# Sliding-window attention feeding a tanh MLP: attention stages spread over half-slots, and the second batch's V loaded later

## The chip, the cores and the metric

One Trainium2 chip, one core. The metric is the device time of one execution in microseconds. A profiled execution gives a trace; its span runs from the first to the last instruction and is a little shorter than the device time.

## The reference, cut to what matters

Eight batches of eight heads, 576 tokens, head size 64. Each token attends to itself and the 63 tokens before it. The attention output, with the heads side by side, is 4608 tokens of 512 channels; it goes through `w_in` (512 x 2048), `h - tanh(h)`, and `w_out` (2048 x 512).

```
B, H, S, D = 8, 8, 576, 64
rel  = pos[:, None] - pos[None, :]
mask = (rel >= 0) & (rel < 64)
attn = softmax(where(mask, q @ k.T / sqrt(D), -1e9))
x    = (attn @ v).transpose(0, 2, 1, 3).reshape(B * S, H * D)
h    = x @ w_in
out  = (h - tanh(h)) @ w_out
```

## The kernel before

**Attention** goes by pairs of heads: `g` counts 32 pairs, four to a batch (`b, pr = divmod(g, 4)`). For one pair: `load_qk` (SP queue) fetches q and k in f32, `cast_qk` (GpSimd) makes bf16 rows, and `tr` transposes them on TensorE (8 transposes for q, 8 for k). For q, ScalarE and then VectorE copy the two halves from PSUM into `qT`; for k ScalarE copies all into `kT`. The 576 queries are nine windows of 64, in three groups of three: `scores(g, grp)` is three matmuls into a PSUM tile and one Exp on ScalarE into `PT`; `masking(g)` is one VectorE multiply over all nine; `pv(g, grp)` is three matmuls with V (whose 129th column of ones gives the row sums) into the one PSUM buffer `ov`, then on VectorE a reciprocal and two multiplies into `xs`. After every second pair `x_tr` transposes four, then five windows of `xs` on TensorE, and VectorE copies them into `xT`, the MLP's input. `kT`, `qT` and `PT` have three buffers each, the transposes' PSUM tile `tp` two.

V sits in `vw` (two buffers, for two batches): `load_v(b)` (GpSimd queue) writes the upper 64 partitions with a cast to bf16, and `shift_v(b)` (SP queue) copies them on the chip to the lower 64 partitions one window further on, so that one matmul sees 128 keys. `pv` needs both.

**The MLP** goes by chunks of 512 tokens (`c` = 0 to 8), 16 steps to a chunk; `n` counts steps over all chunks. A step has `hp_mm(c, m)`: four matmuls with `w_in` into a PSUM tile `hp` (two buffers), Tanh on ScalarE, and the subtraction into `gT` on VectorE; and `yp_mm(c - 1, m)`: four matmuls with `w_out` for the chunk before. Every four steps `y_out` copies a finished `yp` (one PSUM buffer) on ScalarE and stores it. Chunk 0 (n = 0 to 15) has no `yp`, chunk 9 (n = 144 to 159) no `hp`. A chunk is eight windows and a batch nine, so chunk `c` needs the first windows of batch `c` (for c below 8) besides those left of the batch before.

**The order** is written by hand and each engine runs its instructions in that order. At step `n`: `y_out`, `hp_mm`, what stands in the table `early` for this step, `yp_mm`, what stands in `late`. Pair `g` starts at step `a` (from batch 1 on every four steps) and takes five steps: transposes at `a`, scores at `a+1`, mask and first `pv` at `a+2`, the other `pv` at `a+3`, `x_tr` at `a+4`. Mask and first `pv` are neighbours, and so are each `pv` and the `hp` or `yp` between them. Ahead of the loop stand the loads of the first batch: SP has q and k of four pairs and two `shift_v`; GpSimd's queue has V of batch 0, casts and `w_in` in quarters. V of batch 1 comes at step -8, `w_out` in quarters at steps -3 to 0, between casts.

Of the kernel before, what the change touches and what calls it, by code (L numbers as in the profile page):

```python
# [15 lines left out]
def kernel(  # L16
# [11 lines left out]
    NP = H // 2  # L28
    NJ = S // 64
# [6 lines left out]
    NC = NT // TOK  # L36
    M = d_ff // 128
# [17 lines left out]
    mask = const.tile([128, 64], BF16, name="mask")  # L55
# [19 lines left out]
    def cast(eng, g, n):  # L75
        t = row_pool.tile([P, E, 2, D], BF16, tag=n + "b", name=n + "b")
        o = t.rearrange("p e h d -> p h e d")
        i = stage.pop((g, n)).rearrange("p h (e d) -> p h e d", d=D)
        if eng is nc.scalar:
            nc.scalar.activation(o, i, ACT.Copy)  # L80
        else:
            eng.tensor_copy(o, i)  # L82
        rows[g, n] = t

    def cast_qk(g):
        cast(nc.gpsimd, g, "q")
        cast(nc.gpsimd, g, "k")

    def load_v(b, p0=0, p1=NP):
        for i in range(2):  # L90
            nc.gpsimd.dma_start(  # L91
                out=vw[b % NV][64:128, p0:p1, :, 64 * i:64 * i + 64].rearrange("p r j d -> p (r j) d"),
                in_=v[b, NP * i + p0:NP * i + p1].rearrange("h (j p) d -> p (h j) d", p=64))

    def shift_v(b, p0=0, p1=NP):
        w = vw[b % NV].rearrange("p r j c -> p r (j c)")
        nc.sync.dma_start(out=w[0:64, p0:p1, 129:], in_=w[64:128, p0:p1, :(NJ - 1) * 129])
# [23 lines left out]
    def load_w_in(i):  # L121
        nc.gpsimd.dma_start(out=w_in_sb[:, :, 512 * i:512 * i + 512],
                            in_=w_in_r[:, :, 512 * i:512 * i + 512])

    def load_w_out(i):
        nc.gpsimd.dma_start(out=w_out_sb[:, 4 * i:4 * i + 4, :], in_=w_out_r[:, 4 * i:4 * i + 4, :])

    cast(nc.scalar, 0, "q")
    cast(nc.vector, 0, "k")
    shift_v(0, 0, 1)  # L130
    load_v(0, 1, NP)
    cast_qk(1)
    load_w_in(0)
    cast_qk(2)
    shift_v(0, 1, NP)
    load_w_in(1)
    cast_qk(3)
    load_w_in(2)
    load_w_in(3)

    xT = {}

    def chunk_tile(c):
        if c not in xT:
            xT[c] = xt_pool.tile([128, 4, TOK], BF16, tag="xT", name="xT")
        return xT[c]
# [60 lines left out]
    def hp_mm(c, m):  # L207
        hp = ps_hp.tile([128, TOK], F32, tag="hp", name="hp")
        for ki in range(4):
            nc.tensor.matmul(hp, w_in_sb[:, ki, m * 128:(m + 1) * 128], chunk_tile(c)[:, ki, :],  # L210
                             start=(ki == 0), stop=(ki == 3))
        th = sm_pool.tile([128, TOK], F32, tag="th", name="th")
        nc.scalar.activation(th, hp, ACT.Tanh)  # L213
        if m == 0:
            gT[c] = g_pool.tile([128, M, TOK], BF16, tag="gT", name="gT")
        nc.vector.tensor_tensor(gT[c][:, m, :], hp, th, ALU.subtract)  # L216

    def yp_mm(c, st):
        s, part = divmod(st, 4)
        if part == 0:  # L220
            yps[c, s] = ps_yp.tile([128, d_model], F32, tag="yp", name="yp")
        for i in range(4):
            m = 4 * part + i
            nc.tensor.matmul(yps[c, s], gT[c][:, m, s * 128:(s + 1) * 128], w_out_sb[:, m, :],  # L224
                             start=(m == 0), stop=(m == M - 1))

    def y_out(c, s):
        ysb = sm_pool.tile([128, d_model], F32, tag="ysb", name="ysb")
        nc.scalar.activation(ysb, yps[c, s], ACT.Copy)  # L229
        for u in range(2):  # L230
            r0 = c * TOK + s * 128 + 64 * u
            nc.sync.dma_start(out=out[r0:r0 + 64, :].rearrange("(a e) d -> e a d", e=E),
                              in_=ysb[64 * u:64 * u + 64, :])


    early, late = {}, {}

    def at(table, n, *fn):
        table.setdefault(n, []).append(fn)

    NG = B * NP
    LEAD = 18
    for g in range(NG):
        b, pr = divmod(g, NP)
        a = g - 10 if g < NP else 4 * g - LEAD
        if g >= NP:
            at(late, a - 10, load_qk, g)
            at(late, a - 4, cast_qk, g)
        at(early, a, tr, g, "q")
        at(late, a, tr, g, "k")  # L250
        at(early, a + 1, scores, g, 0)
        at(early, a + 1, scores, g, 1)
        at(late, a + 1, scores, g, 2)
        at(early, a + 2, masking, g)
        at(late, a + 2, pv, g, 0)
        at(early, a + 3, pv, g, 1)
        at(late, a + 3, pv, g, 2)
        if pr % 2 == 1:
            at(early, a + 4, x_tr, b, pr // 2, 0, 4)
            at(late, a + 4, x_tr, b, pr // 2, 4, NJ)  # L260
    at(late, -8, load_v, 1)
    at(late, -4, shift_v, 1)
    for i in range(4):
        at(late, -3 + i, load_w_out, i)
    for b in range(2, B):
        a = 4 * (NP * (b - 1) - 1) - LEAD + 4
        at(late, a, load_v, b)
        at(late, a + 9, shift_v, b)

    first = min(min(early), min(late))  # L270
    for n in range(first, 16 * (NC + 1) + 1):
        c, m = divmod(n, M)
        cy, sy = divmod(n - 17, M)
        if n >= 17 and sy % 4 == 3 and cy < NC:
            y_out(cy, sy // 4)
        if 0 <= c < NC:
            hp_mm(c, m)
        for fn in early.get(n, []):
            fn[0](*fn[1:])
        if 1 <= c <= NC:  # L280
            yp_mm(c - 1, m)
        for fn in late.get(n, []):
            fn[0](*fn[1:])

# [1 line left out]
_INS = ['q', 'k', 'v', 'moe_w_in', 'moe_w_out']  # L286
# [26 lines left out]
```

## Time and profile before

| | |
|---|---|
| median of three runs | 490.1 us (489.14 to 490.3) |
| profiled execution, device time | 490.18 us |
| its span | 488.4 us |
| busy: TensorE, VectorE, ScalarE, GpSimd | 356.4, 237.4, 183.5, 91.2 us |
| mean granted TensorE clock | 0.967 |

Busy times are shares of the whole span; the kernel has four parts that differ: a start, in which loads and the first batch's attention run, chunk 0, the middle (n = 16 to 111), in which the MLP and the attention share the engines, and the end, which is MLP alone.

### The profile page before, as it was taken

The page shows a single profiled execution, that of the slowest core. Times are in us where ns is not written, and L with a number is a line of the kernel's source. Part 1 is how long each engine was busy: PE and PEld are TensorE (multiplying, and loading weights), DVE is VectorE, ACT ScalarE, POOL GpSimd, SP SyncE. Part 2 cuts the span into 40 slices and gives each one's busy share as a digit, 9 for nine tenths or more (in the row PEclk, how much of TensorE's full clock was granted, in tenths as well). Part 3 has the DMA queues.
Part 4 walks back from the last instruction along what each step waited for, and adds up shares of the span by engine and source line. Part 5 has one row for each costly group of instructions (what it writes and reads, how often), then busy time and mean ns, then how long its engine had stood idle before and what let it go on. Part 6 is the DMA issues. An engine that isn't in the chain of part 4 may idle for free.

```text
span 488.4 us, 6341 instructions
## 1 busy us (share of the span) xinstructions
PE 356.4 (73%) x2384; PEld 175.4 (36%) x2384; DVE 237.4 (49%) x553; ACT 183.5 (38%) x342; POOL 91.2 (19%) x97
## 2 busy tenths in 40 slices
PE   3024516765778787878787878887877879999985
PEld 2023303433333333333333333333333334444432
DVE  5036414445465656565555565655556555333410
ACT  5122203333344444435344434344444443443410
POOL 7604402103102211231123111311111000000000
PEclk9999999577899999999999999999999999999999
DMA  9999999505954495369629962996222011101112
GB/s 171 113 181 185 108 158 157 130 0 21 29 93 92 81 110 99 86 90 99 110 75 96 93 114 70 101 89 114 70 71 74 19 31 35 36 30 44 43 43 64
DMA packets 58765, 41.84 MB, mean 86 GB/s; under 512 B 38768, under 2 KB 42864, under 8 KB 58736
## 3 DMA queue, kind: packets, MB, share of 16 engines
q0 software_dynamic: 41376, 8.91, 62.7%
q1 hardware_dynamic: 17360, 32.54, 29.0%
q8 instruction: 18, 0.29, 0.3%
q14 instruction: 11, 0.09, 0.1%
HBM read 36.70 MB, written 9.44 MB: 94 GB/s over the span
## 4 chain that ended last, share of the span: by engine, by line
PE 49%; DVE 20%; DMA 13%; ACT 12%; issue 4%; POOL 1%; SPq 1%; ACTq 0%; POOLq 0%
PE hp L210 23%; PE yp L224 15%; DVE gT L216 10%; ACT th L213 8%; DMA vw<-in_v_dram 7%; PE ov L180 4%; DVE xs L186 4%; DVE pt L173 4%; ACT ysb L229 3%; DMA vw<-vw 3%; PE sp L167 3%; PE tp L153 3%; DMA kf<-in_k_dram 3%; DVE xT L200 1%; PE tpx L192 1%
## 5 line engine op out<-in xcount | busy, mean ns | idle before, releaser
L216 DVE TENSOR_TENSOR gT<-hp,th 128x512 bf16<-128x512 f32 x144 | 99.6, 692 | 153.7 <-ACT th L213 153.7
L213 ACT ACTIVATE th<-hp 128x512 f32<-128x512 f32 x144 | 86.1, 598 | 214.5 <-PE hp L210 214.5
L210 PE MATMUL hp<-xT,w_in_sb 128*128 128x512 bf16 x576 | 157.5, 398 | 0.0
L224 PE MATMUL yp<-w_out_sb,gT 128*128 128x512 bf16 x576 | 145.9, 379 | 7.5 <-ACT ysb L229 7.5
L180 PE MATMUL ov<-vw,pt 128*128 128x129 bf16 x288 | 37.3, 242 | 100.7 <-DVE xs L186 41.8
L224 PEld LDWEIGHTS <-gT 128*128 128x128 bf16 x576 | 52.7, 98 | 63.2 <-issue 15.0
L82 POOL CAST qb<-qf 72x1024 bf16<-72x1024 f32 x31 | 32.9, 1061 | 202.3 <-DMA qf<-in_q_dram 168.8
L180 PEld LDWEIGHTS <-pt 128*128 128x128 bf16 x288 | 18.6, 104 | 144.6 <-DVE xs L186 55.0
L186 DVE TENSOR_TENSOR xs<-ov,rc 64x192 bf16<-64x192 f32 x192 | 68.2, 355 | 4.6
L210 PEld LDWEIGHTS <-w_in_sb 128*128 128x128 bf16 x576 | 53.3, 102 | 45.1 <-issue 6.0
L169 ACT ACTIVATE pt<-sp 128x384 bf16<-128x384 f32 x96 | 43.5, 490 | 29.9 <-PE sp L167 28.6
L183 DVE RECIPROCAL rc<-ov 128x3 f32<-128x3 f32 x96 | 17.0, 177 | 60.0 <-PE ov L180 59.8
L82 POOL CAST kb<-kf 72x1024 bf16<-72x1024 f32 x31 | 32.4, 1046 | 13.0 <-DMA kf<-in_k_dram 5.4
L167 PE MATMUL sp<-qt,kt 128*128 128x128 bf16 x288 | 30.5, 241 | 4.7 <-ACT kt L160 2.4
L91 POOL DMA_DIRECT2D vw<-in_v_dram x18 | 19.9, 1113 | 66.9 <-PE ov L180 66.2
L160 ACT ACTIVATE kt<-tp 128x576 bf16<-128x576 bf16 x32 | 20.8, 650 | 24.2 <-PE tp L153 24.2
L167 PEld LDWEIGHTS <-kt 128*128 128x128 bf16 x288 | 21.7, 108 | 22.4 <-ACT kt L160 12.7
L229 ACT ACTIVATE ysb<-yp 128x512 f32<-128x512 f32 x36 | 21.4, 593 | 17.3 <-PE yp L224 17.3
L157 ACT ACTIVATE qt<-tp 64x576 bf16<-64x576 bf16 x32 | 20.3, 636 | 11.1 <-PE tp L153 11.1
L173 DVE TENSOR_TENSOR pt<-pt,mask 128x1152 bf16<-128x1152 bf16 x32 | 24.2, 758 | 0.1
L192 PE MATMUL tpx<-ident,xs 128*128 128x128 bf16 x144 | 15.3, 242 | 6.7 <-DVE xT L200 6.3
L153 PE MATMUL tp<-ident,qb 72*128 72x72 bf16 x256 | 15.9, 213 | 5.5 <-ACT qb L80 5.5
(24 smaller groups left out, 100.2 us busy)
## 6 DMA issues: line engine op xcount, KB each, us to landing
qf<-in_q_dram SPq DMA_DIRECT2D x32, 288.0 KB
kf<-in_k_dram SPq DMA_DIRECT2D x32, 288.0 KB
out_dram<-ysb SPq DMA_DIRECT2D x72, 128.0 KB
vw<-in_v_dram POOLq DMA_DIRECT2D x14, 288.0 KB, 10.8
vw<-vw SPq DMA_DIRECT2D x7, 516.0 KB
w_in_sb<-in_moe_w_in_dram POOLq DMA_DIRECT2D x4, 512.0 KB, 20.2
w_out_sb<-in_moe_w_out_dram POOLq DMA_DIRECT2D x4, 512.0 KB, 21.9
vw<-in_v_dram POOLq DMA_DIRECT2D x2, 216.0 KB, 18.8
```

The source lines that it names most:

```text
L82: eng.tensor_copy(o, i)
L153: nc.tensor.transpose(tp[:, e, :], src[:, e, :], ident[:P, :P])
L167: nc.tensor.matmul(sp[:, i, :], kT[g % NR][:, 64 * j:64 * j + 128], qT[g % NR][:, j].rearrange("c h t -> c (h t)"), start=True, stop=True)
L169: nc.scalar.activation(PT[g % NR][:, 3 * grp:3 * grp + 3, :], sp, ACT.Exp, scale=scale)
L173: nc.vector.tensor_tensor(p, p, mask.unsqueeze(1).to_broadcast([128, 2 * NJ, 64]), ALU.mult)
L180: nc.tensor.matmul(ov[:, i, :], PT[g % NR][:, j, :], vw[b % NV][:, pr, j, :], start=True, stop=True)
L186: nc.vector.tensor_tensor(xs[b % 2][r, 3 * grp:3 * grp + 3, pr, :], ov[r, :, r], rc[r].to_broadcast([64, 3, 64]), ALU.mult)
L210: nc.tensor.matmul(hp, w_in_sb[:, ki, m * 128:(m + 1) * 128], chunk_tile(c)[:, ki, :], start=(ki == 0), stop=(ki == 3))
L213: nc.scalar.activation(th, hp, ACT.Tanh)
L216: nc.vector.tensor_tensor(gT[c][:, m, :], hp, th, ALU.subtract)
L224: nc.tensor.matmul(yps[c, s], gT[c][:, m, s * 128:(s + 1) * 128], w_out_sb[:, m, :], start=(m == 0), stop=(m == M - 1))
L229: nc.scalar.activation(ysb, yps[c, s], ACT.Copy)
```

## The change

Slots become half-slots: `h = 2n` holds `y_out`, `hp_mm` and its items, `h = 2n + 1` holds `yp_mm` and its items, in one table `items`. The VectorE subtraction of a step moves out of `hp_mm` into `g_sub`, which is issued after the items of the even half-slot. A pair of batch 2 or later starts every eight half-slots as before, but is spread over 20 of them (`WIDE`); its batch's last `x_tr` stands at `h = 32b - 1`, the half-slot before chunk `b` begins, and `shift_v(b)` 22 half-slots after `load_v(b)`, twelve ahead of the first `pv` that reads it. Batches 0 and 1 have a tighter list (`TIGHT`, 12 half-slots), a pair every three or four half-slots; batch 1's four pairs now lie wholly within chunk 0 (h = 8 to 31). In the queues, V of batch 1 goes behind all of `w_in` and `w_out`, its `shift_v` stands at h = 6, and V of batch 2 at h = -3.

```diff
     cast(nc.scalar, 0, "q")
     cast(nc.vector, 0, "k")
-    shift_v(0, 0, 1)
     load_v(0, 1, NP)
+    load_w_in(0)
     cast_qk(1)
-    load_w_in(0)
+    load_w_in(1)
     cast_qk(2)
-    shift_v(0, 1, NP)
-    load_w_in(1)
-    cast_qk(3)
     load_w_in(2)
     load_w_in(3)
+    cast_qk(3)
+    for i in range(4):
+        load_w_out(i)
+    load_v(1)
+    shift_v(0, 0, 1)
+    shift_v(0, 1, NP)
...
         nc.scalar.activation(th, hp, ACT.Tanh)
+        return hp, th
+
+    def g_sub(c, m, hp, th):
         if m == 0:
             gT[c] = g_pool.tile([128, M, TOK], BF16, tag="gT", name="gT")
         nc.vector.tensor_tensor(gT[c][:, m, :], hp, th, ALU.subtract)
...
-    LEAD = 18
+    WIDE = dict(q=0, k=1, s0=4, s1=4, s2=6, mask=8, v0=10, v1=13, v2=15, x0=17, x1=19)
+    TIGHT = dict(q=0, k=1, s0=3, s1=3, s2=4, mask=5, v0=6, v1=7, v2=8, x0=10, x1=11)
+    at_v2 = {}
     for g in range(NG):
         b, pr = divmod(g, NP)
-        a = g - 10 if g < NP else 4 * g - LEAD
-        if g >= NP:
-            at(late, a - 10, load_qk, g)
-            at(late, a - 4, cast_qk, g)
...
+        o = TIGHT if b < 2 else WIDE
+        a = 3 * g - 21 if b == 0 else 4 * g - 8 if b == 1 else 8 * g - 44
+        if b > 0:
+            at(a - 24, load_qk, g)
+            at(a - 8, cast_qk, g)
+        at(a + o["q"], tr, g, "q")
+        at(a + o["k"], tr, g, "k")
+        for i in range(3):
+            at(a + o[f"s{i}"], scores, g, i)
+        at(a + o["mask"], masking, g)
+        for i in range(3):
+            at(a + o[f"v{i}"], pv, g, i)
+        at_v2[g] = a + o["v2"]
         if pr % 2 == 1:
...
+            at(a + o["x0"], x_tr, b, pr // 2, 0, 4)
+            at(a + o["x1"], x_tr, b, pr // 2, 4, NJ)
+    at(6, shift_v, 1)
     for b in range(2, B):
...
+        a = at_v2[NP * (b - 1) - 1] + 1
+        at(a, load_v, b)
+        at(a + 22, shift_v, b)
+
+    for h in range(min(items), 2 * 16 * (NC + 1) + 2):
+        n = h // 2
         c, m = divmod(n, M)
...
+        if h % 2 == 0:
+            cy, sy = divmod(n - 17, M)
+            if n >= 17 and sy % 4 == 3 and cy < NC:
+                y_out(cy, sy // 4)
+            if 0 <= c < NC:
+                hidden = hp_mm(c, m)
+        elif 1 <= c <= NC:
+            yp_mm(c - 1, m)
+        for fn in items.get(h, []):
             fn[0](*fn[1:])
...
+        if h % 2 == 0 and 0 <= c < NC:
+            g_sub(c, m, *hidden)
```

## Rows read from the trace of the kernel before

**Rows 1.** The page: granted TensorE clock (tenths) and GB/s in 40 slices.
```profile
PEclk9999999577899999999999999999999999999999
GB/s 171 113 181 185 108 158 157 130 0 21 29 93 92 81 110 99 86 90 99 110 75 96 93 114 70 101 89 114 70 71 74 19 31 35 36 30 44 43 43 64
```

**Rows 2.** The waits, whole span: total us, times, longest us.
```profile
PE ov L180 <- DVE xs L186: 41.8, 63, 2.0
PE ov L180 <- DVE pt L173: 29.3, 28, 2.1
```

**Rows 3.** Timeline of TensorE in the middle: start, duration, instruction, [idle before].
```profile
203.61 0.35 PE L180 MATMUL ov<-vw,pt 128*128 128x129 bf16 x3 [0.88 <-DVE xs L186]
203.80 1.02 PE L210 MATMUL hp<-xT,w_in_sb 128*128 128x512 bf16 x4
204.66 0.42 PE L153 MATMUL tp<-ident,qb 72*128 72x72 bf16 x8
204.92 1.03 PE L224 MATMUL yp<-w_out_sb,gT 128*128 128x512 bf16 x4
...
206.96 0.51 PE L167 MATMUL sp<-qt,kt 128*128 128x128 bf16 x6
207.30 1.03 PE L224 MATMUL yp<-w_out_sb,gT 128*128 128x512 bf16 x4
...
214.92 0.35 PE L180 MATMUL ov<-vw,pt 128*128 128x129 bf16 x3 [0.88 <-DVE xs L186]
...
215.97 0.39 PE L192 MATMUL tpx<-ident,xs 128*128 128x128 bf16 x4
216.19 0.42 PE L153 MATMUL tp<-ident,qb 72*128 72x72 bf16 x8
```

**Rows 4.** Windows: busy us of each engine in eight steps of the middle (two pairs).
```profile
207.47:231.35 23.88, 19.21 (x142) 9.23 (x141) 13.83 (x33) 10.41 (x21) 5.82 (x6) 1.00 1.67 97
```

**Rows 5.** Groups by line over the whole span: busy us, mean ns of one | idle before.
```profile
L216 DVE TENSOR_TENSOR gT<-hp,th 128x512 bf16<-128x512 f32 x144 | 99.6, 692 | 153.7 <-ACT th L213 153.7
L213 ACT ACTIVATE th<-hp 128x512 f32<-128x512 f32 x144 | 86.1, 598 | 214.5 <-PE hp L210 214.5
...
L173 DVE TENSOR_TENSOR pt<-pt,mask 128x1152 bf16<-128x1152 bf16 x32 | 24.2, 758 | 0.1
...
L158 DVE COPY qt<-tp 64x576 bf16<-64x576 bf16 x32 | 14.7, 461 | 6.3 <-ACT qt L157 5.4
```

**Rows 6.** Timeline: shift of batch 1, steps 0, 16, 112 and 113.
```profile
56.59 0.60 SPq L97 DMA_DIRECT2D vw<-vw  x1
...
57.58 1.91 PE L210 MATMUL hp<-xT,w_in_sb 128*128 128x512 bf16 x4
...
71.43 0.38 PE L180 MATMUL ov<-vw,pt 128*128 128x129 bf16 x2 [9.58 <-DMA vw<-vw]
...
125.29 1.06 PE L210 MATMUL hp<-xT,w_in_sb 128*128 128x512 bf16 x4
...
410.42 1.03 PE L210 MATMUL hp<-xT,w_in_sb 128*128 128x512 bf16 x4
...
412.14 1.03 PE L210 MATMUL hp<-xT,w_in_sb 128*128 128x512 bf16 x4
```

**Rows 7.** V of batch 1: instruction ns and issue times, then issue to landing.
```profile
L91 POOL DMA_DIRECT2D vw<-in_v_dram x2: 1180/1183/1186, 19.1 to 20.2; - x2
...
DMA to landing us min/median/max: 33.2/34.7/36.3
```

**Rows 8.** Windows of the DMA: granted clock, share of 16 engines, GB/s.
```profile
42.00:44.00 2.00, 1.00 1.10 255
...
50.00:52.00 2.00, 1.00 4.22 52
...
197.00:199.00 2.00, 1.00 0.01 2
```

**Rows 9.** SP's queue: a shift in the middle.
```profile
188.04 0.66 SPq L97 DMA_DIRECT2D vw<-vw  x1
```

More of the change, by code (lines that the diff above doesn't have):

```diff
@@ L233, in y_out, with at @@
                               in_=ysb[64 * u:64 * u + 64, :])
-    early, late = {}, {}
-    def at(table, n, *fn):
-        table.setdefault(n, []).append(fn)
+    items = {}
+    def at(h, *fn):
+        items.setdefault(h, []).append(fn)
     NG = B * NP
-    LEAD = 18
+    WIDE = dict(q=0, k=1, s0=4, s1=4, s2=6, mask=8, v0=10, v1=13, v2=15, x0=17, x1=19)
+    TIGHT = dict(q=0, k=1, s0=3, s1=3, s2=4, mask=5, v0=6, v1=7, v2=8, x0=10, x1=11)
+    at_v2 = {}
     for g in range(NG):
         b, pr = divmod(g, NP)
-        a = g - 10 if g < NP else 4 * g - LEAD
-        if g >= NP:
-            at(late, a - 10, load_qk, g)
-            at(late, a - 4, cast_qk, g)
[L249 to L257, printed above, removed]
-        if pr % 2 == 1:
-            at(early, a + 4, x_tr, b, pr // 2, 0, 4)
-            at(late, a + 4, x_tr, b, pr // 2, 4, NJ)
@@ L261 @@
[L261 to L264, printed above, removed]
-    for b in range(2, B):
[L266 to L271, printed above, removed]
-        c, m = divmod(n, M)
[L273 to L278, printed above, removed]
+        o = TIGHT if b < 2 else WIDE
@@ L279 @@
             fn[0](*fn[1:])
[L280 to L283, printed above, removed]
+        if h % 2 == 0 and 0 <= c < NC:
+            g_sub(c, m, *hidden)
 _INS = ['q', 'k', 'v', 'moe_w_in', 'moe_w_out']
```

## The prediction

> **What bounds the kernel now.** The page's strips come first, since the kernel is four kernels in a row. In [rows 1] the granted clock dips between the seventh and the tenth slice (about 85 to 125 us) and is full from there on, and the DMA is busy until about 95 us, then nearly still: a start that is ruled by loads, and a middle that is not. The timeline gives the borders [rows 6]: step 0 starts at 57.58, step 16 (the first with both MLP matmuls) at 125.29, step 112 (the first without attention) at 410.42; the span ends at 488.4. So 57.6 us go to the first batch, 67.7 to chunk 0, 285.1 to the 96 middle steps, 78.0 to the end.
>
> The end shows what TensorE takes for a step: two steps from 410.42 to 412.14, so 1.72 us are one step and 0.86 four matmuls [rows 6]. A middle step takes 285.1/96 = 2.97, or 11.88 for four steps, which hold one pair. What of this is TensorE's own? I read it from starts, since the durations overlap [rows 3]: a `pv` group delays its successor by 203.80 - 203.61 = 0.19, eight transposes by 204.92 - 204.66 = 0.26, six score matmuls by 207.30 - 206.96 = 0.34, four `x_tr` by 216.19 - 215.97 = 0.22. A pair then has 3 x 0.19 + 2 x 0.26 + 1.5 x 0.34 + 0.25 (nine `x_tr` for two pairs) = 1.85, and four steps need 4 x 1.72 + 1.85 = 8.73. The other 3.15 us are waits.
>
> The waits name them [rows 2]: `pv` for the multiplies that empty `ov` (41.8 us in 63 waits) and for the mask (29.3 in 28). Two neighbours in the order meet there: TensorE asks for the mask one matmul group after VectorE began it, behind a subtraction that itself waits for Tanh (153.7 us of VectorE's idle time [rows 5]). No engine is full: in two pairs' 23.88 us VectorE works 13.83, ScalarE 10.41 [rows 4]. So the middle is bound by the order, and if the order were free, by TensorE at 8.73, with VectorE at 6.9 a pair behind it.
>
> **The middle, changed.** A period is eight half-slots. I place its work by the offset from the q transposes: mask of the pair before and q at 0, k (and `x0` of an odd pair) at 1, first `pv` at 2, `x1` at 3, two score groups at 4, second `pv` at 5, third score group at 6, third `pv` at 7. Follow TensorE from the start of `hp` at 0, with no waits: the first `pv` comes two `hp`, one `yp` and two sets of transposes later, at 3 x 0.86 + 0.52 = 3.1. VectorE has by then done the mask: it starts after the third `pv`'s multiplies of the period before, which end about 1.2 after this `hp` starts (an estimate from the 0.88 wait behind a group like it [rows 3]), so at about 2.0 with the mask's 0.76 [rows 5]. The second `pv` comes 2.9 after the first and the third 2.1 after the second; a group with its multiplies is through in about 1.3 (0.19 + 0.2 to get going + 0.88), and one subtraction of 0.69 in front still fits. The moved subtraction holds `hp`, which has two buffers, so it is due two steps later, at 4.2. At offset 0 it is last: `hp` done at 1.02, Tanh 1.62, ScalarE's q copy 2.3 (as long as the transposes' other copies, an estimate), VectorE's q copy 0.46, subtraction 0.69: 3.45. It fits by 0.7.
>
> Two things do not fit. In a period with `x0`, the k transposes need the `tp` buffer of q (two buffers, three users in one step): free at 2.8, wanted at 2.2, so 0.6 lost in every second period, 11.5 x 0.6 = 7 us. And a batch's last `x_tr` stands in the half-slot before the chunk that reads it: VectorE has `pv`'s multiplies and a subtraction (0.9 + 0.69) in its queue before the copies (0.56, an estimate of two or three short copies), TensorE arrives right after the transposes; I take 1.1 us for each of six chunks, 6.6 us (0 to 1.6 each).
>
> Of the 24 pairs, 22.9 by work lie behind step 16. Floor: 96 x 1.72 + 22.9 x 1.85 = 207.5. With the two losses **221** (2.30 a step), against 285.1. Low end 207.5; high end, half of today's waits back, 207.5 + 24 x 1.57 = 245.
>
> **Loads in the middle.** A load of q and k has 16 half-slots (18 us) before its cast. The V shift has only twelve half-slots, 6 x 2.30 = 13.8 us, before its first reader. Its cover: one issued at 188.04 had left the DMA still by 197 [rows 8, 9], so at most 9 us. If it took what it took in the start (below, 14.8), TensorE would wait 1.0 in each of six batches. I take nothing, high end 6 us.
>
> **The start and chunk 0.** V of batch 1 was issued last at 20.2 and landed 36.3 later, at 56.5 [rows 7]; its shift went at 56.59 and the waiting `pv` at 71.43 [rows 6], 14.8 for the shift beside other loads. Now four quarters of `w_out` stand before it in the same queue, 0.52 MB each. Low: at 255 GB/s, what DMA gave at 42 to 44 us [rows 8], 2.1 us each, 8 in all. High: at 108, the slowest of the first eight slices [rows 1], 4.9 each, 19. I take 13.5, nearer to neither, because q and k of five pairs run beside them: V lands at 70. The shift behind it: 9 to 14.8; V of batch 2 is on the move then, in small pieces (52 GB/s at 50 to 52 us [rows 8]), so 13. It lands at **83** (74 to 91). SP stands at the wait for V meanwhile, with q and k of pair 10 behind it, which nobody needs before half-slot 36.
>
> The reader, `pv` of pair 4, is at half-slot 14. Step 0 I leave at 57.6, because V of batch 0, its shifts and the serial groups behind them are as before; seven `hp` at 1.9 [rows 6] and the transposes bring TensorE to half-slot 14 at about 73. It waits there some 10 us, so up to 10 us more in the first batch cost nothing.
>
> From there to step 16 VectorE has nine subtractions (6.2) and the attention of about four pairs: a pair without subtractions is (13.83 - 8 x 0.69)/2 = 4.15 [rows 4, 5], with the parts of pairs 8 and 9 and without what is done of 4 and 5 some 17.5. Together 24, the low end. TensorE at half clock (`hp` four in 1.9 with its fill, 1.72 without [rows 6]) needs 9 x 1.72 + 4.2 x 3.7 = 31. With no `yp` between them the tight list's mask, `pv` and reciprocal alternate on the two engines; I take 33 (24 to 40). Step 16 starts at 83 + 33 = **116** (before: 125.3), of which a dip of the granted clock like the one at 85 to 125 us [rows 1] is part.
>
> **The sum.** 116 + 221 + 78.0 = 415 of span. The profiled run took 1.8 more than its span (490.18 against 488.4) and stands 0.1 above the median: **417 us**, 15% less. Removed instructions: none; added: none.
>
> **A rule against it.** TensorE was granted the full clock through all of the middle, although it idles there [rows 1]; 2.4 GHz, the upper of its two levels. The Trainium skill, "TensorE: Matmul & The Clock Gate", section "A second HAM failure mode: psum-queue depth-cycling", says that short idles between groups that rotate through PSUM can let the clock go back and forth; by that rule the new order, which rotates more such tiles at once, could pay half-clock stretches. The trace before disagrees, with more idle time than I expect. The same page's section "Back-to-back issue gap" states about 131 ns for a matmul of 512 columns in a stream; the end's rows show 1.72/8 = 215, and the measurement decides.
>
> **The rivals.**
> - *Half of the waits come back* at other places (the `tp` buffers, the q copy that waits for ScalarE's, the chunk borders): for it, six or seven producers and consumers per period within 0.7 us of each other; against, each slack above is positive. 116 + 245 + 78 + 1.8 = 441.
> - *The DMA cannot follow.* Four pairs move 97 GB/s x 47.8 us = 4.6 MB [rows 4]; in 36.9 us that is 126 GB/s. The first eight slices gave 108 to 185 [rows 1]. At 108 a batch takes 43, 6 us more for each of six: 417 + 36 = 453.
> - *Slower: the clock.* If TensorE falls to 1.2 GHz in the middle, four steps need 17.5 instead of 8.7. The gain of 73 us is gone when 73/8.7 = 8.4 of the 24 periods run so; half of them gives 417 + 12 x 8.7 = 521. Against it: [rows 1].
> - *TensorE's pace isn't the floor* (its matmuls stream faster than the end shows, where ScalarE and VectorE would set the pace): then VectorE's 6.9 a pair is, 116 + 24 x 6.9 + 7 + 78 + 2 = 369.
> - *No change:* the waits only move, 490.
>
> **How the numbers follow.** Forecast 0.76 (its own range 400 to 433), half of the waits 0.11, DMA 0.06, clock 0.03, faster floor 0.02, no change 0.02. A shift that lands 9 us off either way moves the forecast by as much. The range of 400 to 440 leaves out the DMA, the clock, the fast floor, no change and part of the half waits. Faster: 0.76 + 0.11 + 0.06 + 0.02 = 0.95; same (within 0.3%, 1.5 us, about what three runs of this kernel spread over) 0.02; slower 0.03.
>
> **What would show it.** Right: middle steps at 2.2 to 2.4 us; waits for the mask and for `ov` gone after step 16; `pv` of pair 4 released by the shift near 83; step 16 near 116; the end 78.0 as before. Wrong: `hp` waiting for the subtraction; k transposes or a chunk's first `hp` waiting more than 1.5; `pv` waiting for a shift in later batches; a granted clock under 1 after 130 us. The number fails first at the landing of V, which I know only within 17 us.

## The result, and the profile after

The changed kernel takes 415.35 us (415.04 to 415.48, four runs) against 490.2: a ratio of 0.8475 (0.8461 to 0.849). The forecast was 417, range 400 to 440, faster. In experiments 5, 6 and 10 one or two runs fell into a slower state: the medians and ranges given there hold these runs, the ratios leave them out.

The page of the profiled execution, whose span is 413.3 us: busy time of each engine, the granted clock in tenths over 40 slices, and the shares of the chain that ended last.

```profile
PE 328.9 (80%) x2384; PEld 179.0 (43%) x2384; DVE 241.5 (58%) x553; ACT 185.5 (45%) x342; POOL 90.7 (22%) x97
...
PEclk9999797558989999999999999999999999999999
...
PE 64%; DMA 18%; DVE 9%; ACT 4%; issue 2%; POOL 1%; ACTq 0%; SPq 0%; POOLq 0%
```

The same line on the page of the kernel before:

```profile
PE 49%; DVE 20%; DMA 13%; ACT 12%; issue 4%; POOL 1%; SPq 1%; ACTq 0%; POOLq 0%
```

The busy times of VectorE, ScalarE and GpSimd hardly change, TensorE's falls from 356.4 to 328.9 us. In the chain the shares of VectorE and ScalarE fall from 20 and 12% to 9 and 4%; it is now TensorE with a DMA piece. Where that piece lies shows the timeline of TensorE: start, duration, instruction, and in brackets the idle time before it and what ended it.

```profile
50.80 3.42 PE L213 MATMUL hp<-xT,w_in_sb 128*128 128x512 bf16 x8
...
73.65 0.27 PE L183 MATMUL ov<-vw,pt 128*128 128x129 bf16 x1 [10.81 <-DMA vw<-in_v_dram]
84.88 0.38 PE L183 MATMUL ov<-vw,pt 128*128 128x129 bf16 x2 [10.96 <-DMA vw<-vw]
...
115.23 0.38 PE L213 MATMUL hp<-xT,w_in_sb 128*128 128x512 bf16 x1 [0.28 <-DVE gT L222]
117.39 0.81 PE L213 MATMUL hp<-xT,w_in_sb 128*128 128x512 bf16 x3 [1.78 <-DVE xT L203]
...
118.37 1.80 PE L230 MATMUL yp<-w_out_sb,gT 128*128 128x512 bf16 x4
...
155.70 0.81 PE L213 MATMUL hp<-xT,w_in_sb 128*128 128x512 bf16 x3 [0.59 <-DVE xT L203]
...
192.92 0.81 PE L213 MATMUL hp<-xT,w_in_sb 128*128 128x512 bf16 x3 [0.53 <-DVE xT L203]
...
335.26 1.03 PE L213 MATMUL hp<-xT,w_in_sb 128*128 128x512 bf16 x4
```

Step 0 starts at 50.80; V of batch 1 lands at 73.65 and its shift at 84.88, and the `pv` of pair 4 waits for both; step 16 starts at 115.23 and step 112 at 335.26. The middle takes 220.0 us in place of 285.1 [rows 6], the end 78.0 as before.

One period with `x0` and one without, in the middle:

```profile
205.47 1.03 PE L213 MATMUL hp<-xT,w_in_sb 128*128 128x512 bf16 x4
206.33 0.42 PE L156 MATMUL tp<-ident,qb 72*128 72x72 bf16 x8
206.59 1.03 PE L230 MATMUL yp<-w_out_sb,gT 128*128 128x512 bf16 x4
207.46 0.39 PE L195 MATMUL tpx<-ident,xs 128*128 128x128 bf16 x4
208.20 0.42 PE L156 MATMUL tp<-ident,kb 72*128 72x72 bf16 x8 [0.36 <-DVE qt L161]
...
214.95 1.02 PE L213 MATMUL hp<-xT,w_in_sb 128*128 128x512 bf16 x4
...
223.41 1.02 PE L213 MATMUL hp<-xT,w_in_sb 128*128 128x512 bf16 x4
```

From 205.47 to 214.95 are 9.48 us, from there to 223.41 are 8.46; before, a period took 11.88. The only bracket left is that of the k transposes behind `x0`. The waits view of TensorE between 130 and 330 us (total us, times, longest), first two lines of the kernel before, then all lines of the changed one:

```profile
PE ov L180 <- DVE xs L186: 17.9, 34, 0.9
PE ov L180 <- DVE pt L173: 13.8, 16, 0.9
...
PE tp L156 <- DVE qt L161: 5.9, 11, 1.0
PE hp L213 <- DVE xT L203: 1.1, 2, 0.6
```

The waits of [rows 2], which are those of the whole span, are gone from the middle; what is left of them (9.2 and 8.1 us) lies in the first two batches.

### The profile page after: what moved, and what is told of

It is laid out like the page before. It is cut to its first block, busy times and chain, and to the rows that moved or that the text cites. A ratio compares the mean times of both kernels' runs of the same rounds, so it can differ in the third digit from the quotient of the medians.

```text
span 413.3 us, 6323 instructions
## 1 busy us (share of the span) xinstructions
PE 328.9 (80%) x2384; PEld 179.0 (43%) x2384; DVE 241.5 (58%) x553; ACT 185.5 (45%) x342; POOL 90.7 (22%) x97
## 4 chain that ended last, share of the span: by engine, by line
PE 64%; DMA 18%; DVE 9%; ACT 4%; issue 2%; POOL 1%; ACTq 0%; SPq 0%; POOLq 0%
PE yp L230 27%; PE hp L213 26%; DMA vw<-in_v_dram 10%; DMA w_in_sb<-in_moe_w_in_dram 5%; PE ov L183 4%; PE sp L170 3%; DMA vw<-vw 3%; PE tp L156 3%; DVE xs L189 2%; DVE pt L176 2%; DVE gT L222 2%; ACT th L216 2%; DVE qt L161 2%; ACT qt L160 1%; POOL vw L91 1%
## 5 line engine op out<-in xcount | busy, mean ns | idle before, releaser
L213 PE MATMUL hp<-xT,w_in_sb 128*128 128x512 bf16 x576 | 152.4, 387 | 4.0 <-DVE xT L203 2.9
L183 PE MATMUL ov<-vw,pt 128*128 128x129 bf16 x288 | 35.5, 235 | 56.5 <-DMA vw<-vw 21.5
L183 PEld LDWEIGHTS <-pt 128*128 128x128 bf16 x288 | 23.8, 103 | 80.8 <-issue 47.1
L170 PEld LDWEIGHTS <-kt 128*128 128x128 bf16 x288 | 23.3, 107 | 13.7 <-ACT kt L163 1.8
L176 DVE TENSOR_TENSOR pt<-pt,mask 128x1152 bf16<-128x1152 bf16 x32 | 28.1, 877 | 0.9
L161 DVE COPY qt<-tp 64x576 bf16<-64x576 bf16 x32 | 14.7, 460 | 13.2 <-ACT qt L160 13.0
L156 PE MATMUL tp<-ident,kb 72*128 72x72 bf16 x256 | 14.8, 205 | 7.9 <-DVE qt L161 6.9
```

What stands on the lines that cost most here:

```text
L156: nc.tensor.transpose(tp[:, e, :], src[:, e, :], ident[:P, :P])
L170: nc.tensor.matmul(sp[:, i, :], kT[g % NR][:, 64 * j:64 * j + 128], qT[g % NR][:, j].rearrange("c h t -> c (h t)"), start=True, stop=True)
L176: nc.vector.tensor_tensor(p, p, mask.unsqueeze(1).to_broadcast([128, 2 * NJ, 64]), ALU.mult)
L183: nc.tensor.matmul(ov[:, i, :], PT[g % NR][:, j, :], vw[b % NV][:, pr, j, :], start=True, stop=True)
```

## The experiments

In all tables and lists below, "middle" is from the start of step 16 to that of step 112. The intervals are of the ratio to the kernel before, timed on the same chip.

**1. The subtraction moved, alone.** Into the kernel before, with `hp_mm` split into `hp_mm` and `g_sub` as in the change:

```diff
...
-            hp_mm(c, m)
+            hidden = hp_mm(c, m)
         for fn in early.get(n, []):
             fn[0](*fn[1:])
+        if 0 <= c < NC:
+            g_sub(c, m, *hidden)
```

> The kernel before, with nothing changed but the place of the subtraction: it is issued after the early items of its step. Theory (the middle loses time because the mask and the multiplies stand on VectorE behind a subtraction that waits for Tanh, next to the pv that needs them): part of the wait goes without any spacing. Mask done 1.5 us after its step's hp starts, pv at 1.7: no wait; the second and third pv still meet their neighbours, 0.6 and 0.3 us. Waits of a pair fall from 3.15 to about 1.4 us; 24 pairs give 36 to 42 us: 448 to 458 us. Rival (only distance in half-slots takes the waits away): 485 to 490 us.

Measured: 429.61 us, ratio 0.875 (0.8705 to 0.8795), far below the theory's range: this edit is worth more than the theory gave it. Its timeline in the middle, TensorE and VectorE, and the waits line for `ov` between 130 and 330 us:

```profile
213.90 0.76 DVE L173 TENSOR_TENSOR pt<-pt,mask 128x1152 bf16<-128x1152 bf16 x1 [0.62 <-ACT pt L169]
...
215.27 0.34 PE L180 MATMUL ov<-vw,pt 128*128 128x129 bf16 x3
...
216.64 0.35 PE L180 MATMUL ov<-vw,pt 128*128 128x129 bf16 x3 [0.17 <-DVE xs L186]
...
218.03 0.35 PE L180 MATMUL ov<-vw,pt 128*128 128x129 bf16 x3 [0.17 <-DVE xs L186]
```

```profile
PE ov L180 <- DVE xs L186: 7.1, 40, 0.2
```

Mask and `pv` are still neighbours in the order, and the mask is on time all the same: VectorE no longer waits for Tanh ahead of it. The two later groups wait 0.17 where [rows 3] had 0.88. Since durations overlap, a bracket understates a loss: from 216.64 to 218.03 are 1.39 us, where a `pv` and four matmuls delay by 0.19 + 0.86 = 1.05, so each of the two loses 0.34. Over 24 pairs that makes 16 us (an estimate from these rows), most of what the distances still save. Middle 238.5, step 16 at 112.75. A part of the gain up to step 16 goes with TensorE's clock: from the shift's landing to step 16 the mean granted clock is 0.92 here (71.67 to 112.75) and 0.72 before (71.43 to 125.29).

**2. The subtraction back at its place, the rest as changed.**

```diff
-                hidden = hp_mm(c, m)
+                g_sub(c, m, *hp_mm(c, m))
...
-        if h % 2 == 0 and 0 <= c < NC:
-            g_sub(c, m, *hidden)
```

> The changed kernel with the subtraction back at its old place, right behind Tanh; spacing, start and loads as changed. Theory: distance covers a late mask; only the q copy comes later, and with it the k transposes of every second pair, 1.4 us of wait in place of 0.5: 11 us more, 3 more in chunk 0, 426 to 432 us. Rival (the moved subtraction carries the gain, the spacing little): above 450 us.

Measured: 438.77 us, ratio 0.8939 (0.891 to 0.8969); middle 244.2. It lies between the theory's range and the rival's. The place was right (the k transposes wait 21.1 us in ten waits, up to 3.7), the size was not: 24 us in the middle, not 11, and step 16 only 0.3 later, not 3. The timeline of VectorE, GpSimd and TensorE about the longest of these waits:

```profile
188.32 2.29 POOL L91 DMA_DIRECT2D vw<-in_v_dram  x2 [14.20 <-PE ov L183]
...
190.05 3.20 DVE L176 TENSOR_TENSOR pt<-pt,mask 128x1152 bf16<-128x1152 bf16 x1
190.59 1.06 POOL L82 CAST qb<-qf 72x1024 bf16<-72x1024 f32 x1
191.57 1.05 POOL L82 CAST kb<-kf 72x1024 bf16<-72x1024 f32 x1
192.56 1.58 POOL L82 CAST qb<-qf 72x1024 bf16<-72x1024 f32 x1
193.28 0.46 DVE L161 COPY qt<-tp 64x576 bf16<-64x576 bf16 x1
...
193.79 0.42 PE L156 MATMUL tp<-ident,kb 72*128 72x72 bf16 x8 [3.67 <-DVE qt L161]
194.04 1.84 PE L213 MATMUL hp<-xT,w_in_sb 128*128 128x512 bf16 x4
```

The mask, 0.76 elsewhere, takes 3.20 while GpSimd issues the V load and casts, and the third cast, 1.04 elsewhere, takes 1.58, as if the two could not run at the same time. Three masks of the middle take 3.2 us. The clock adds to it: behind this wait `hp` takes 1.84 where others take 1.03, and the granted clock from 194 to 200 us is 0.72, so TensorE runs a part of that stretch at the lower of its two levels.

**3. The old distances, subtraction still moved.**

```diff
-    WIDE = dict(q=0, k=1, s0=4, s1=4, s2=6, mask=8, v0=10, v1=13, v2=15, x0=17, x1=19)
+    WIDE = dict(q=0, k=1, s0=2, s1=2, s2=3, mask=4, v0=5, v1=6, v2=7, x0=8, x1=9)
...
-        a = 3 * g - 21 if b == 0 else 4 * g - 8 if b == 1 else 8 * g - 44
+        a = 3 * g - 21 if b == 0 else 4 * g - 8 if b == 1 else 8 * g - 36
```

> The changed kernel with the old distances for the pairs of batches 2 to 7 (scores two half-slots after the transposes, mask and pv neighbours, x_tr eight and nine after), subtraction still moved, start and loads as changed. Theory: a pair's waits come back by 0.9 us for pv and the tp waits stay, 18 to 24 us over 24 pairs: 433 to 440 us. Rival (distance is all): the middle returns to 285 us, 475 to 480 us. Second rival (distance is worth nothing once the subtraction has moved): 415 us.

Measured: 431.84 us, ratio 0.8812 (0.8774 to 0.8849); middle 239.0, nearly that of experiment 1 (238.5), whose start is the old one. Neither rival holds, and the theory is 1.2 us off the low end of its range, by other waits than it named: the `tp` waits are gone, and between 130 and 330 us `pv` waits for `ov` 40 times, never over 0.2. Middle times of the four combinations:

| | subtraction behind Tanh | subtraction moved |
|---|---|---|
| old distances | 285.1 (before) | 238.5 (experiment 1) |
| new distances | 244.2 (experiment 2) | 220.0 (the change) |

Each alone takes 41 to 47 us off, both together 65: they remove largely the same waits.

**4. V behind the weights, alone, in the kernel before.**

```diff
     load_w_in(2)
     load_w_in(3)
+    for i in range(4):
+        load_w_out(i)
+    load_v(1)
...
-    at(late, -8, load_v, 1)
...
-    for i in range(4):
-        at(late, -3 + i, load_w_out, i)
```

> The kernel before with V of batch 1 put behind w_in and w_out in the queue and nothing else. Theory (the queue's order decides when the shift lands, and pv of pair 4 waits for it): V lands near 73 and the shift near 85 in place of 71.4, all that follows is later by about 13 us: 500 to 506 us. Rival (hidden behind the first batch, or the weights that come earlier give it back): 488 to 492 us.

Measured: 495.94 us, ratio 1.0108 (1.0074 to 1.0141): 1% slower, 5 us and not 13; both ranges are missed.

```profile
65.47 0.27 PE L183 MATMUL ov<-vw,pt 128*128 128x129 bf16 x1 [10.80 <-DMA vw<-in_v_dram]
77.23 0.38 PE L183 MATMUL ov<-vw,pt 128*128 128x129 bf16 x2 [11.49 <-DMA vw<-vw]
```

V lands at 65.5 and not at 73, and the shift releases `pv` at 77.2, 5.8 later than in [rows 6]; step 16 starts 4.5 later, the middle is 285.1 again. The theory's sign holds. Its landing time was taken from the changed kernel, which issues the q and k loads of five pairs between 27 and 60 us; this run issues three, and V, issued at the same times (28.8 and 31.4 us), lands 8 us earlier. That these loads are the cause is not shown.

**5. V ahead of `w_out`** (still behind `w_in`), in the changed kernel.

```diff
+    load_v(1)
     for i in range(4):
         load_w_out(i)
-    load_v(1)
```

> The changed kernel with V of batch 1 ahead of w_out in the queue (still behind w_in). Theory (pv of pair 4 waits for V and its shift, and nothing else holds chunk 0 there): V lands near 53, the shift near 66 in place of 84.9, step 16 near 97 in place of 115.2: 395 to 400 us. Rival (the load of all data or w_out for step 16 holds the start): 410 to 415 us.

Measured: 404.3 us (399.52 to 406.23), ratio 0.8229 (0.817 to 0.8289); between the two ranges; the profiled run, at 399.52, is the fastest of the four. Lines of its timeline, TensorE and SP's queue:

```profile
39.23 0.37 PE L183 MATMUL ov<-vw,pt 128*128 128x129 bf16 x2 [4.93 <-DMA vw<-vw]
...
56.50 5.58 PE L213 MATMUL hp<-xT,w_in_sb 128*128 128x512 bf16 x15 [0.52 <-DVE xT L203]
...
59.53 0.60 SPq L97 DMA_DIRECT2D vw<-vw  x1
...
72.96 0.38 PE L183 MATMUL ov<-vw,pt 128*128 128x129 bf16 x2 [2.46 <-DMA vw<-vw]
```

SP issues the shift at 59.53, when V has landed, and not at 73.57 as in the changed kernel: `w_out` ahead of V costs 14.0 us. The wait of pair 4 is nearly gone, but the first batch is 5.7 later, because the second shift of its own V comes only at 39.2 (in the changed kernel no `pv` waits for it). In that run step 16 starts at 101.4.

**6. The first `x_tr` one half-slot later**, in the changed kernel.

```diff
-    WIDE = dict(q=0, k=1, s0=4, s1=4, s2=6, mask=8, v0=10, v1=13, v2=15, x0=17, x1=19)
+    WIDE = dict(q=0, k=1, s0=4, s1=4, s2=6, mask=8, v0=10, v1=13, v2=15, x0=18, x1=19)
```

> The changed kernel with the first x_tr of batches 2 to 7 one half-slot later, so that it no longer stands between the q and the k transposes of a later pair. Theory (two tp buffers, three users in one step): the k transposes' wait of 0.5 us in twelve periods goes, 5 to 7 us: 408 to 411 us. Rival (the wait moves to the second x_tr or to the score matmuls): 414 to 416 us.

Measured: 409.23 us (406.17 to 413.18), ratio 0.839 (0.8335 to 0.8444), in the theory's range; middle 213.7 in place of 220.0. In the middle's waits of TensorE the k transposes no longer appear:

```profile
PE hp L213 <- DVE xT L203: 1.6, 2, 0.8
```

**7. Experiments 5 and 6 together.**

> The changed kernel with V of batch 1 ahead of w_out and the first x_tr of batches 2 to 7 one half-slot later, both at once. Theory (one saves in chunk 0, the other in the middle, so they add): 404.3 less 6, 395 to 400 us. Rival (the start decides and the middle waits elsewhere): 402 to 405 us.

Measured: 396.98 us, ratio 0.8107 (0.8075 to 0.8138). They add: 415.35 less 11.05 and 6.12 is 398.2.

**8. V held back until the cast of pair 4**, `x_tr` later too.

```diff
-    for i in range(4):
-        load_w_out(i)
-    load_v(1)
...
-            at(a - 8, cast_qk, g)
+            at(-13 if g == NP else a - 8, cast_qk, g)
...
+    at(-12, load_v, 1)
+    for i in range(4):
+        at(-11, load_w_out, i)
```

> As the run with V of batch 1 ahead of w_out and x_tr later, but V of batch 1 is issued only after the cast of pair 4 (near 37 us in place of 18), w_out behind it. Theory (V issued early, although queued behind w_in, slows the second shift of batch 0, from 34 to 39 us of landing, and the first hp from 51 to 56): the first hp returns to 51, V lands near 54, its shift near 66, step 16 near 95 to 98: 388 to 394 us. Rival (the early V is not what slows that shift): first hp at 56 as in that run, 396 to 400 us.

Measured: 397.7 us, ratio 0.8119 (0.8085 to 0.8154), no better than 7: in the rival's range, but not by its condition, an `hp` at 56. Half of the theory holds: no `pv` waits for the first batch's second shift, and the first `hp` comes at 53.0 in place of 57.1 in experiment 7. But V, issued at 40, landed only at 66, 26 us later. Standing behind `w_in` accounts for 4 us of that at most: the last quarter was issued by 16.1, and none took more than 27.7 us to land, so `w_in` was in by 43.8. What held V up after that stays open.

```profile
66.16 0.22 PE L180 MATMUL ov<-vw,pt 128*128 128x129 bf16 x1 [2.03 <-DMA vw<-in_v_dram]
74.63 0.37 PE L180 MATMUL ov<-vw,pt 128*128 128x129 bf16 x2 [8.25 <-DMA vw<-vw]
```

**9. The old start under the new middle.** The changed kernel with the queue order of before (V of batch 1 at once behind `w_in`, `w_out` later) and the old places of batches 0 and 1 (the reordering ahead of the loop, which goes back to the kernel before, is left out here):

```diff
...
-    TIGHT = dict(q=0, k=1, s0=3, s1=3, s2=4, mask=5, v0=6, v1=7, v2=8, x0=10, x1=11)
+    TIGHT = dict(q=0, k=1, s0=2, s1=2, s2=3, mask=4, v0=5, v1=6, v2=7, x0=8, x1=9)
...
-        a = 3 * g - 21 if b == 0 else 4 * g - 8 if b == 1 else 8 * g - 44
+        a = 2 * g - 20 if b == 0 else 8 * g - 36 if b == 1 else 8 * g - 44
...
-            at(a - 24, load_qk, g)
-            at(a - 8, cast_qk, g)
+            at(a - 19 if b == 1 else a - 24, load_qk, g)
+            at(a - 7 if b == 1 else a - 8, cast_qk, g)
...
-    at(6, shift_v, 1)
+    at(-15, load_v, 1)
+    at(-7, shift_v, 1)
+    for i in range(4):
+        at(2 * i - 5, load_w_out, i)
```

> The changed kernel with the queue order and the schedule of batches 0 and 1 of the kernel before; the subtraction stays moved and batches 2 to 7 keep their new distances. Theory (the new start gains nothing: V behind the weights costs in chunk 0 what the tight schedule saves): step 16 near 113 as with the subtraction moved alone, the middle 220: 410 to 414 us. Rival (the own schedule of the first batches carries part of the gain): 425 us or more.

Measured: 407.37 us, ratio 0.8317 (0.8285 to 0.8349): 8 us faster than the whole change, and below the theory's range. Step 16 starts at 111.0 and the middle takes 216.3, 3.7 less than in the changed kernel. Two losses of the changed kernel have no counterpart here: the 1.78 behind 115.23, and the lower level of the clock right behind it (granted 0.50 from 119 to 121 us; the `yp` at 118.37 takes 1.80 and not 1.03), which here is granted in full from 110 to 122. The run takes back the queue order and the tight schedule together; what the schedule alone is worth no run shows.

```profile
69.84 0.38 PE L180 MATMUL ov<-vw,pt 128*128 128x129 bf16 x2 [9.06 <-DMA vw<-vw]
```

**10. V ahead of the second half of `w_in`**, issued after the cast of pair 4, its shift at half-slot -5, `x_tr` later as in experiment 6:

```diff
-    load_w_in(2)
-    load_w_in(3)
     cast_qk(3)
-    for i in range(4):
-        load_w_out(i)
-    load_v(1)
...
-            at(a - 8, cast_qk, g)
+            at(-13 if g == NP else a - 8, cast_qk, g)
...
-    at(6, shift_v, 1)
+    at(-12, load_v, 1)
+    for i in range(2, 4):
+        at(-12, load_w_in, i)
+    for i in range(4):
+        at(-12, load_w_out, i)
+    at(-5, shift_v, 1)
```

> The changed kernel with x_tr later as before, and V of batch 1 issued after the cast of pair 4 (near 37 to 40 us), ahead of the second half of w_in and all of w_out; its shift stands at half-slot -5. Theory (pv of pair 4 waits for V and its shift alone, the rest of the weights can come behind them): V lands near 51, the shift near 62, before half-slot 14 is reached (67); no wait there, step 16 near 95: 386 to 390 us. Rival (the total of the loads binds: w_in's second half then comes too late for steps 8 to 15, or the clock stays low in chunk 0): 394 to 400 us.

Measured: 386.27 us (384.08 to 393.33), ratio 0.7857 (0.7818 to 0.7896), in the theory's range and the fastest here. SP could issue the shift at 51.5, so V had landed by then, and pair 4's first `pv` waits for its mask, not for a load:

```profile
51.52 0.60 SPq L97 DMA_DIRECT2D vw<-vw  x1
```

```profile
63.53 0.35 PE L178 MATMUL ov<-vw,pt 128*128 128x129 bf16 x3 [1.91 <-DVE pt L171]
...
92.08 0.28 PE L178 MATMUL ov<-vw,pt 128*128 128x129 bf16 x2 [2.12 <-DMA vw<-vw]
```

Step 16 starts at 92.5, the middle is 212.8; at 92.08 the next batch's shift is the one waited for, 2.1 us.

## Why the prediction was right, and where it was not

**The middle** was forecast at 221 and took 220.0, in part by luck: two of its terms missed, and the misses nearly cancel. The floor of 8.73 a period that came out of the starts in [rows 3] is there: 8.46 without `x_tr`, where the forecast's terms give 8.48. (One distance was summed wrong: by the same terms the second `pv` comes 3.1 after the first, not 2.9, and the trace has 3.10; nothing hung on it.) The `tp` loss, 7 us in the sum, is 5.9 in the waits and 6.3 by experiment 6. Its size was right, its make-up only in part: eight of the eleven waits are 0.36, and three are 1.01, in the periods in which the mask takes 1.60 and not 0.76 (last section).

The loss at the chunk borders, 6.6 in the sum, is the term that failed. The forecast counted six chunks whose first `hp` reads a batch's last `x_tr`, but by the windows (chunk `c` has 8c to 8c + 7, the last `x_tr` of batch `b` 9b + 4 to 9b + 8) only chunks 2 and 3 read one; chunks 4 to 7 need no window of it. The trace has these two waits and no third: 0.59 at 155.70 and 0.53 at 192.92, 1.1 together. In its place stand two losses at step 16 that the sum did not have: chunk 1, a border outside the forecast's six, waits 1.78 for the `x_tr` of batch 1, and TensorE's clock is at its lower level right behind it (experiment 9), together about 3.6 by the starts of the rows. The 1.78 is also over the 1.5 that the forecast named as a sign of being wrong.

**Chunk 0** was forecast by V and its shift: 70, 83 and 116, measured 73.65, 84.88 and 115.2. Here too errors cancel: V lands 3.7 late, the shift takes 11.2 and not 13, and from its landing to step 16 are 30.3 and not 33. The price of `w_out` ahead of V, 13.5 in the sum, is 14.0 by experiment 5. The term that was free to be wrong is the start of step 0: I left it at 57.6 "because V of batch 0, its shifts and the serial groups behind them are as before", and it was 50.8. The second shift of batch 0 is not as before. In the kernel before and in experiments 1, 5, 7 and 9, which issue V of batch 1 between 17 and 23 us, `pv` waits for that shift until 38.8 to 39.9 us; in all others, which issue V at 28.5 us or later, no `pv` waits for it. Since pair 4 waits for V in any case, the 7 us were lost again in the idle time at half-slot 14, as the forecast said of that slack, though it was 21.8 us and not some 10. How a V load that stands behind `w_in` slows an earlier shift stays open.

**What carries the gain** the forecast did not see. It named the subtraction that waits for Tanh among the causes of the waits, but put the middle's gain down to the order as a whole, and treated the moved subtraction as something that must fit, by 0.7 us, not as a gain. Experiment 1 shows that this edit alone brings 46.6 of the middle's 65 and starts step 16 12.5 earlier; the distances add 18.5 to 19 more when it is there (experiments 1 and 3), and bring 40.9 when it isn't (experiment 2). And the edits of the start cost: with the old start the kernel is 8 us faster (experiment 9), V behind the weights alone makes the kernel before 1% slower (experiment 4), and in the changed kernel V's place is worth 11 us ahead of `w_out` and, further forward with its shift and ahead of half of `w_in`, another 11 (experiment 5, and 7 against 10). So 417 was near because the price of a late V, 83 us for its shift, stood in the sum.

**Two readings of the kernel before** were off, without moving the forecast. The DMA is not "nearly still" after 95 us: in [rows 1] it is so for three slices, and then moves 70 to 114 GB/s through most of the middle, as the forecast's own DMA rival has it. And [rows 2] is the whole span; between 130 and 330 us the two waits are 17.9 and 13.8 us.

**The rivals.** Half of the waits back: no, between 130 and 330 us 7 us of waits are left. The DMA: it moved 102 GB/s over the middle and no `pv` waited for a V or a shift there. The clock: granted in full from 130 us to the end of the middle; in experiment 2, where TensorE waits up to 3.7 us, it falls in the middle, so that rival's price is real, but its condition did not come about in the changed kernel. TensorE's pace is the floor: VectorE was busy 166 us of the 218 from 117.4 to 335.3.

## What to carry to other kernels

Look first for an in-order engine that waits for another at the head of its queue while ready work stands behind: moving that one instruction behind the ready work took 61 us here, before any distance was changed. Distances and moved instructions remove the same waits, so price them together, as a table of both, and not one after the other. In a start that loads bind, order the queue by first use: 590 KB of V ahead of 3 MB of weights that are read later, with its shift as early, was worth 23 us (experiment 6 against 10).

## What the runs showed of the hardware that had not been expected

VectorE's mask multiply reads two SBUF tiles, and GpSimd can hold it up. It takes 0.76 us alone and 3.20 in experiment 2, when two casts follow the issue of a V load. The multiplies that read PSUM kept their 0.36 us in the same stretches. The Trainium skill, "SBUF — State Buffer", section "SBUF: two separate sides", has the rule for the casts: a VectorE operation with two SBUF inputs and a GpSimd operation that reads SBUF exclude each other for the whole instruction. The 3.20 agrees. In the changed kernel the issue of a V load alone, 2.29 us, does it too, but not always: of four masks that meet it in the middle three take 1.60 and end as it ends, and one takes its usual 0.76. What decides is open.

```profile
150.26 2.29 POOL L91 DMA_DIRECT2D vw<-in_v_dram  x2 [13.97 <-PE ov L183]
150.80 0.76 DVE L176 TENSOR_TENSOR pt<-pt,mask 128x1152 bf16<-128x1152 bf16 x1
...
186.76 2.29 POOL L91 DMA_DIRECT2D vw<-in_v_dram  x2 [14.17 <-PE ov L183]
187.43 1.60 DVE L176 TENSOR_TENSOR pt<-pt,mask 128x1152 bf16<-128x1152 bf16 x1
```

Loads on GpSimd's queue wait for earlier ones: with ten issued, the next two each waited for a V load to land, and the two after them for parts of `w_in`, so that V of batch 1, last in the order, was issued at 28.8 and 31.4 us and not at 20. In the order of the queue the load waited for is each time the eighth before. Whether that is a limit of the queue or of the semaphores with which the program was built, no run tells. The changed kernel's GpSimd queue:

```profile
22.06 0.74 POOL L126 DMA_DIRECT2D w_out_sb<-in_moe_w_out_dram  x1 [2.65 <-DMA vw<-in_v_dram]
26.67 0.74 POOL L126 DMA_DIRECT2D w_out_sb<-in_moe_w_out_dram  x1 [3.87 <-DMA vw<-in_v_dram]
28.79 1.17 POOL L91 DMA_DIRECT2D vw<-in_v_dram  x1 [1.38 <-DMA w_in_sb<-in_moe_w_in_dram]
31.41 1.15 POOL L91 DMA_DIRECT2D vw<-in_v_dram  x1 [1.45 <-DMA w_in_sb<-in_moe_w_in_dram]
```
